# Moving the routing to odd steps, the token sums ahead of their splits, and two stored-square jobs into the next block, in a hand-ordered attention and mixture kernel

## The chip, the cores and the metric

The kernel runs on one core of a Trainium2 chip. The metric is device microseconds for one execution. Three runs of the kernel before gave a median of 723.92 us (723.49 to 724.7).

## The reference

Three layers follow one another on 3072 tokens with 512 features:

```
attention  4 batches, 8 heads, chunks of 32 queries, 8 memory + up to 56 context keys
dense      h = x @ w_in (512 x 2048); g = s * relu(h)^2 + b; y = g @ w_out (2048 x 512)
soft MoE   logits = y @ phi (32 slots); d = softmax over all 3072 tokens; slots = d.T @ y
           8 experts on 4 slots each: relu(slots @ w1[e]) @ w2[e]
           out = softmax over the slots(logits) @ slot_out
```

All data are float32.

## The kernel before

The tokens are cut into six planes of 512 (j = 0 to 5). For the dense layer each float32 operand is split into a high and a low part (ACT writes the high part with a copy, DVE or POOL subtracts it to get the low part), and each product is three matmuls (high x high, high x low, low x high). One matmul has a 128x128 stationary and a 128x512 moving operand.

Planes 0 and 1 run in 32 plain steps (16 tiles of the 2048 middle features for each plane). Step n issues on PE: 12 matmuls of `mm_h(n)` (L326, writes HB[n % 2]), then background work, then 12 matmuls of `mm_y(n-1)` (L345, accumulates in banks 0 to 3). On ACT and DVE `make_g(n)` turns h into the two parts of g, and `split_wi`, `split_wo` make the weights' parts for coming steps (two buffers each, wi0/wi1 and wo0/wo1). The background work is the attention of a later plane and the routing of the plane before, given by the table `bg`. Attention of one head pair is "qk" (32 small matmuls, L192, then exp and norm on DVE and ACT), two steps later "tr" (four transposes L221, `att_place` copies them to pb), one step later "pv" (32 small matmuls L241 and a copy L247). Routing is "log" (logits L371, running maximum, exp), "etr" (two transposes), four "ytr" (four transposes each, L393, and one copy to SBUF), "csoft" (DVE and ACT only) and "slot" (8 matmuls L409). "tr", "qk" and routing alternate over banks 6 and 7 through `mbank()`.

Planes 2 and 3, then 4 and 5, go through `super_block(s)`, s = 0 and 1. There eight pairs of feature tiles, p = 0 to 7, each form h with seven products instead of eight (`prod`, L630, 6 matmuls each, in the order a11, s1, s2, s4, s3, a22, a12 on the four banks A to D). Its operands are the token sums `x_sum` (t1 to t4, built in place from the raw tokens x0h), split by `x_split` into w0 to w13, and the weight sums `w_sums`, split by `w_split`. Two of the four resulting squares are used at once for the first plane's y (two jobs of 12 matmuls L345, run one pair later from the list `pending`), two are stored (x1h, sp0 to sp3). After the pairs come 16 "stored-square jobs" (`t2_job(i)`, L345), 12 matmuls each, for the second plane. `prep(i)` splits the weights and squares for job i: `wo_split` (L635 on ACT, L636 on POOL) and `g_split` (L643 on ACT, L647 on DVE). While the jobs of block 0 run, `tasks` make the sums and splits of block 1. Routing of a finished plane stands at spots (p, k): k = 1 after product s2, k = 2 after product s3; k = 1 uses bank B, k = 2 bank D.

What sets the order: the steps before 28 have PE and SP ordered by hand, with ACT, DVE and POOL placed by a scheduler; from step 28 to the end of both blocks the order of the program is the order on all five queues. Each engine takes its queue strictly in order. The expert layer after the blocks is not touched.

Of the kernel before, what the change touches and what calls it, by code (L numbers as in the profile page):

```python
# [38 lines left out]
def tile_attention_moe_softmoe(  # L39
# [524 lines left out]

    def x_split(op, s, kt):
        j = NPL + 2 * s
        t = hl(fresh(f"w{XO[op] + kt}"))
        src = {"b21": xraw(j, 2 + kt), "b22": xraw(j + 1, 2 + kt), "t3": xraw(j + 1, kt)}.get(op, xraw(j, kt))
        act.activation(out=r32(t[:, 0]), in_=src, func=AF.Copy)
        dve.tensor_tensor(out=r32(t[:, 1]), in0=src, in1=t[:, 0], op=ALU.subtract)  # L570
# [84 lines left out]
    def super_block(s, pending):  # L655
# [106 lines left out]
        if s == 0:  # L762
            for kt in range(2):
                task(1 + kt, x_split, "b11", 1, kt)
                task(1 + kt, x_sum, "t1", 1, kt)
                task(1 + kt, x_split, "t1", 1, kt)
                task(3 + kt, x_sum, "t3", 1, kt)
                task(3 + kt, x_sum, "t2", 1, kt)
                task(4 + kt, x_split, "t2", 1, kt)
                task(6 + kt, x_split, "b22", 1, kt)  # L770
                task(6 + kt, x_sum, "t4", 1, kt)
                task(8 + kt, x_split, "b21", 1, kt)
                task(11 + kt, x_split, "t3", 1, kt)
                task(13 + kt, x_split, "t4", 1, kt)
            task(8, wi_load, 0)
            task(10, w_sums, 0)
# [404 lines left out]
```

## Time and profile before

| | us |
|---|---|
| median of three runs | 723.92 |
| the profiled execution | 728.35 |
| its span on the chip | 726.6 |
| PE busy (modelled) | 673.3 |
| DVE, ACT, POOL busy | 420.5, 380.3, 308.3 |

The stretches of the program in this execution: plain steps 16 to 31 from about 126 to 272 us, pairs of block 0 to 424, its stored-square jobs to 489, pairs of block 1 to 616, its jobs to 670, experts and output to the end. A row of the timeline has start, length, engine, line, operation, output and inputs, and in brackets the idle time of that engine just before with what ended it. PE is the engine to follow: a bracket on a PE row is time lost if nothing later has slack. A matmul row's length includes a latency of the last matmul, so the next row can start a little before the end of the one above.

### The profile page before, as it was taken

The page shows a single profiled execution, that of the slowest core. Times are in us where ns is not written, and L with a number is a line of the kernel's source. Part 1 is how long each engine was busy: PE and PEld are TensorE (multiplying, and loading weights), DVE is VectorE, ACT ScalarE, POOL GpSimd, SP SyncE. Part 2 cuts the span into 40 slices and gives each one's busy share as a digit, 9 for nine tenths or more (in the row PEclk, how much of TensorE's full clock was granted, in tenths as well). Part 3 has the DMA queues.
Part 4 walks back from the last instruction along what each step waited for, and adds up shares of the span by engine and source line. Part 5 has one row for each costly group of instructions (what it writes and reads, how often), then busy time and mean ns, then how long its engine had stood idle before and what let it go on. Part 6 is the DMA issues. An engine that isn't in the chain of part 4 may idle for free.

```text
span 726.6 us, 12554 instructions
## 1 busy us (share of the span) xinstructions
PE 673.3 (93%) x4983; PEld 527.3 (73%) x4983; DVE 420.5 (58%) x692; ACT 380.3 (52%) x688; POOL 308.3 (42%) x261
## 2 busy tenths in 40 slices
PE   6899999988899779999999998888999999999996
PEld 3678887776678666787777886666787887877474
DVE  4799997544454534656655555864354446464423
ACT  3898874544344444554555554536464456353323
POOL 4100001322244475665666436886396674253000
PEclk8999999999899989999999999999999999999998
DMA  8999946641223502433321050003922100999896
GB/s 338 397 373 343 392 146 199 192 152 65 87 88 117 203 29 88 145 132 134 142 88 59 30 203 30 0 30 107 383 71 76 59 30 29 386 353 344 319 361 266
DMA packets 37786, 126.90 MB, mean 175 GB/s; under 512 B 4192, under 2 KB 4192, under 8 KB 37728
## 3 DMA queue, kind: packets, MB, share of 16 engines
q1 hardware_dynamic: 37728, 126.11, 47.1%
q8 instruction: 39, 0.64, 0.4%
q14 instruction: 19, 0.16, 0.1%
HBM read 111.41 MB, written 14.68 MB: 174 GB/s over the span
## 4 chain that ended last, share of the span: by engine, by line
PE 69%; DVE 10%; ACT 6%; POOL 6%; issue 5%; DMA 2%; SPq 0%; DVEq 0%; ACTq 0%; POOLq 0%
PE bank L345 30%; PE bank L630 15%; PE bank L326 9%; PE bank L241 3%; PE bank L192 2%; DVE rt L653 2%; PE bank L1043 2%; PE bank L1002 2%; POOL x00n L576 1%; DMA v<-vd 1%; POOL wo L636 1%; PE bank L393 1%; ACT rt L650 1%; POOL x01n L576 1%; POOL sp6n L603 1%
## 5 line engine op out<-in xcount | busy, mean ns | idle before, releaser
L345 PE MATMUL bank<-g,wo 128*128 128x512 f32 x1008 | 254.4, 403 | 6.1 <-POOL wo L636 4.7
L345 PEld LDWEIGHTS bank<-g,wo 128*128 128x128 f32 x1008 | 188.6, 192 | 52.2 <-POOL wo L636 6.0
L326 PE MATMUL bank<-x,wi 128*128 128x512 f32 x384 | 95.8, 399 | 4.3 <-ACT x03n L247 4.0
L326 PEld LDWEIGHTS bank<-x,wi 128*128 128x128 f32 x384 | 73.5, 193 | 20.7 <-ACT x03n L247 4.5
L636 POOL TENSOR_TENSOR wo<-yt,wo 128x512 fp32r<-128x512 f32 x36 | 49.8, 1387 | 48.5 <-ACT wo L635 48.3
L310 POOL TENSOR_TENSOR wi<-w,wi 128x512 fp32r<-128x512 f32 x16 | 20.5, 1281 | 115.2 <-ACT wi L306 114.0
L333 DVE SCALAR_TENSOR_TENSOR rt<-bank,cons,rt 128x512 f32<-128x512 f32 x32 | 23.9, 747 | 56.2 <-ACT rt L332 56.1
L319 POOL TENSOR_TENSOR wo<-w,wo 128x512 fp32r<-128x512 f32 x16 | 20.8, 1302 | 59.8 <-ACT wo L318 59.8
L623 POOL TENSOR_TENSOR w14n<-sp6n,w14n 128x512 fp32r<-128x512 f32 x16 | 29.6, 1847 | 37.1 <-ACT w14n L622 37.1
L650 ACT ACTIVATE rt1n<-y 128x1024 f32<-128x1024 f32 x16 | 17.0, 1061 | 43.1 <-DVE y L727 43.1
L635 ACT ACTIVATE wo<-yt 128x512 fp32r<-128x512 f32 x36 | 22.7, 631 | 24.8 <-PE bank L345 24.8
L647 DVE SCALAR_TENSOR_TENSOR g<-rt,cons,g 128x512 fp32r<-128x512 f32 x32 | 26.2, 819 | 15.7 <-ACT g L643 15.4
L306 ACT ACTIVATE wi<-w 128x512 fp32r<-128x512 f32 x32 | 20.1, 628 | 27.5 <-PE bank L326 27.5
L318 ACT ACTIVATE wo<-w 128x512 fp32r<-128x512 f32 x32 | 20.2, 632 | 27.2 <-PE bank L345 26.5
L643 ACT ACTIVATE g<-rt,cons 128x512 fp32r<-128x512 f32 x32 | 23.2, 726 | 19.8 <-DVE rt L653 19.8
L192 PEld LDWEIGHTS bank<-k,q 128*64 128x64 f32 x704 | 22.7, 140 | 10.6 <-DVE pb L234 4.1
L241 PEld LDWEIGHTS bank<-pb,v 128*64 128x64 f32 x704 | 23.0, 141 | 10.1 <-issue 4.9
L192 PE MATMUL bank<-k,q 128*64 128x64 f32 x704 | 25.6, 227 | 3.9 <-DVE pb L234 2.2
L725 DVE TENSOR_TENSOR y<-bank,y 128x512 f32<-128x512 f32 x16 | 11.1, 691 | 30.6 <-PE bank L630 30.5
L335 DVE SCALAR_TENSOR_TENSOR g<-rt,cons,g 128x512 fp32r<-128x512 f32 x32 | 25.0, 781 | 6.1 <-ACT g L334 5.5
L653 DVE SCALAR_TENSOR_TENSOR rt<-bank,cons,rt 128x512 f32<-128x512 f32 x16 | 12.0, 750 | 28.2 <-ACT rt L650 28.2
L241 PE MATMUL bank<-pb,v 128*64 128x64 f32 x704 | 26.0, 228 | 1.6 <-DVE x L257 1.4
(487 smaller groups left out, 1541.9 us busy)
## 6 DMA issues: line engine op xcount, KB each, us to landing
sp<-wd SPq DMA_DIRECT2D x24, 512.0 KB, 9.0
k<-kd SPq DMA_DIRECT2D x22, 512.0 KB, 5.7
v<-vd SPq DMA_DIRECT2D x22, 512.0 KB, 4.3
q<-qd SPq DMA_DIRECT2D x20, 512.0 KB, 4.2
yt<-dwo SPq DMA_DIRECT2D x18, 512.0 KB, 3.3
dwi<-w SPq DMA_DIRECT2D x16, 256.0 KB, 7.2
dwo<-w SPq DMA_DIRECT2D x16, 256.0 KB, 6.8
sp4n<-dwi SPq DMA_DIRECT2D x8, 512.0 KB, 3.2
```

What stands on the lines that cost most here:

```text
L192: pe.matmul(S[64 * par:64 * par + 64, 2 * i + z, :], lhsT=qt[:, c].rearrange("p h n -> p (h n)"), rhs=kt[:, c, :], start=True, stop=True)
L241: pe.matmul(b[64 * h:64 * h + 64, 64 * m:64 * m + 64], lhsT=vt[:, m, h, :], rhs=pb[:, m // 2, m % 2, h].rearrange("p z n -> p (z n)"), sta ...
L326: pe.matmul(HB[n % 2], lhsT=r32(w[:, a, kt, :]), rhs=r32(x[:, b]), start=(kt == 0 and i == 0), stop=(kt == 3 and i == 2))
L333: dve.scalar_tensor_tensor(out=t, in0=HB[n % 2], scalar=s_col, in1=r, op0=ALU.mult, op1=ALU.mult)
L335: dve.scalar_tensor_tensor(out=r32(g[:, 1]), in0=t, scalar=b_col, in1=g[:, 0], op0=ALU.add, op1=ALU.subtract)
L345: pe.matmul(yb[dt], lhsT=r32(w[:, a, dt * 128:dt * 128 + 128]), rhs=r32(g[:, b]), start=(first and i == 0), stop=(last and i == 2))
L623: pool.tensor_tensor(out=r32(lo), in0=src, in1=hi, op=ALU.subtract)
L630: pe.matmul(b, lhsT=r32(wv[:, a, kt, :]), rhs=r32(xv[:, c]), start=(first and kt == 0 and i == 0), stop=(kt == 1 and i == 2), skip_group_c ...
L636: pool.tensor_tensor(out=r32(t[:, 1]), in0=src, in1=t[:, 0], op=ALU.subtract)
L647: dve.scalar_tensor_tensor(out=r32(g[:, 1]), in0=t, scalar=b_col, in1=g[:, 0], op0=ALU.add, op1=ALU.subtract)
L650: act.activation(out=r, in_=h, func=AF.Relu, scale=1.0 / WSCALE ** 2)
L653: dve.scalar_tensor_tensor(out=out, in0=h, scalar=s_col, in1=r, op0=ALU.mult, op1=ALU.mult)
```

## The change

1. Routing of plane 0 stands on odd steps (19, 21, 23, 25), beside "pv", instead of even ones (18, 20, 22, 24), beside "tr" and "qk".
2. Steps 28 to 31 have a step of their own, `hand_step`. The split of the weights wi for step n + 2 follows `make_g(n)`; in the old step the split for n + 1 stands at the head of step n. The token sums t2, t3, t4 stand one step ahead of their splits, most of them on DVE instead of POOL; the weight splits of pair 0 are spread over steps 30 and 31. The last "pv" uses bank 7.
3. In a pair, `att_place` stands before `finish`, and the routing spots are one later: (1,1) to (4,1) instead of (0,2) to (3,2).
4. In the stored-square jobs `prep` runs three jobs ahead instead of two, the eight token sums of block 1 move from POOL to DVE one or more jobs before their splits, and the splits are in another order. The raw weights of jobs 10 to 15 swap their tiles.
5. The stored-square jobs 14 and 15 of block 0 run as the two "pending" jobs in pair 0 of block 1, followed by the copy of y to SBUF.

```diff
-    for step, task in ((2, "log"), (2, "ytr0"), (4, "etr"), (4, "ytr1"), (6, "ytr2"), (6, "ytr3"), (6, "csoft"), (8, "slot")):
+    for step, task in ((3, "log"), (3, "ytr0"), (5, "etr"), (5, "ytr1"), (7, "ytr2"), (7, "ytr3"), (7, "csoft"), (9, "slot")):
...
-    WOR = ["yt0", "yt1", "w14", "wi0", "w15", "rt0", "y1", "y0"]
+    WOR = ["yt0", "yt1", "w14", "wi0", "w15", "y0", "y1", "rt0"]
...
-    def x_sum(op, s, kt):
+    def x_sum(op, s, kt, eng=dve):
...
-        pool.tensor_tensor(out=o, in0=a, in1=b, op=ALU.subtract)
+        eng.tensor_tensor(out=o, in0=a, in1=b, op=ALU.subtract)
...
-        routing = {(0, 2): "log", (1, 1): "ytr0", (1, 2): "etr", (2, 1): "ytr1", (2, 2): "ytr2", (3, 1): "ytr3",
-                   (3, 2): "slot"}
+        routing = {(1, 1): "log", (1, 2): "ytr0", (2, 1): "etr", (2, 2): "ytr1", (3, 1): "ytr2", (3, 2): "ytr3",
+                   (4, 1): "slot"}
...
+            if s == 0 and p == 0:
+                x_split("t4", 0, 1)
             if p:
-                finish(p - 1)
                 if s == 0:
                     att_place(4 * NHP + p, D)
+                finish(p - 1)
...
+            for i, op, kt in ((1, "t1", 0), (2, "t1", 1), (4, "t2", 0), (5, "t2", 1), (6, "t3", 0), (7, "t3", 1),
+                              (8, "t4", 0), (9, "t4", 1)):
+                task(i, x_sum, op, 1, kt)
...
+        rest = []
         for i in range(NF):
+            if s == 0 and i >= NF - 2:
+                rest.append(lambda i=i: t2_job(i))
+                continue
             t2_job(i, (3, 2, 0, 1) if i == 0 else (0, 1, 2, 3))
...
+            if i + 3 < NF - 2:
+                prep(i + 3)
+            elif NF - 4 <= i < NF - 2:
+                prep(i + 2)
...
-            if i + 2 < NF:
-                prep(i + 2)
...
+        def hand_step(n):
+            m = n - (NSTEP - 4)
+            if m == 0:
+                split_wi(n + 1)
...
+            split_wo(n)
+            mm_h(n, (0, 1, 2, 3))
+            if m == 3:
+                w_split(1, 0)
+            make_g(n)
+            if n + 2 < NSTEP:
+                split_wi(n + 2)
+            for task, a in bg[n]:
+                run_bg(task, a, bank[7] if n == NSTEP - 1 else HB[(n + 1) % 2] if task == "pv" else mbank())
+            mm_y(n - 1)
+            if m == 0:
+                x_sum("t2", 0, 0, pool)
+                x_sum("t3", 0, 0, pool)
+                x_high("b22", 0, 0)
+            elif m == 1:
+                x_low("b22", 0, 0)
+                x_split("t2", 0, 0)
+                x_split("t3", 0, 0)
+                x_sum("t4", 0, 0)
...
-            super_block(0, [last_plain, lambda: None])
-            super_block(1, [lambda: y_evac(yb=bank[4:8]), lambda: None])
+            rest = super_block(0, [last_plain, lambda: None])
+            super_block(1, [rest[0], lambda: last_jobs(rest[1])])
```

Three places show what this moves. The first is PE in step 18, where the logits (L371) and the first transposes (L393) of the routing stood behind the transposes of the attention (L221, bank 7, `bank_166`) and its "qk" (L192, bank 6, `bank_165`):

```order
 L221 MATMUL bank_166<-cons,ep 128x128 x4
 L192 MATMUL bank_165<-k_102,q_100 64x64 x16
-L371 MATMUL bank_166<-yt_107,cons 32x128 x8
-L371 MATMUL bank_166<-yt_108,cons 32x128 x8
-L393 MATMUL bank_165<-cons,yt_107 128x128 x2
-L393 MATMUL bank_165<-cons,yt_108 128x128 x2
 L345 MATMUL bank_159<-g_96,wo_86 128x512
```

They leave that step, and PE goes from "qk" straight to the job. In step 19 they stand behind "pv" (L241), in the same two banks:

```order
 L326 MATMUL bank_164<-x_94,wi_84 128x512 x3
 L241 MATMUL bank_163<-pb_105,v_103 64x64 x16
+L371 MATMUL bank_166<-yt_107,cons 32x128 x8
+L371 MATMUL bank_166<-yt_108,cons 32x128 x8
+L393 MATMUL bank_165<-cons,yt_107 128x128 x2
+L393 MATMUL bank_165<-cons,yt_108 128x128 x2
 L345 MATMUL bank_159<-g_95,wo_85 128x512
```

One job and one `mm_h` now lie between the users of each bank. The second place is ACT in steps 28 and 29, before. L569 is the high part of an `x_split` (w12 belongs to t4), L306 and L318 are the high parts of the step weights wi and wo, L332 and L334 belong to `make_g`, L247 is the copy of a "pv":

```order
L569 ACTIVATE w8n<-x02n 128x512
L569 ACTIVATE w6n<-x00n 128x512
L569 ACTIVATE w10n<-x00n 128x512
L569 ACTIVATE w12n<-x00n 128x512
L306 ACTIVATE wi_83<-w_81 128x512
L318 ACTIVATE wo_86<-w_80 128x512
L332 ACTIVATE rt_98<-bank_164 128x512
L334 ACTIVATE g_96<-rt_98,cons 128x512
L247 ACTIVATE x03n<-bank_163 128x512
L306 ACTIVATE wi_84<-w_82 128x512
L318 ACTIVATE wo_85<-w_81 128x512
```

The split of t4 stands ahead of the weights of step 30 (`wi_83`) and of the copy x03. Now, from the weights of step 30 on:

```order
L306 ACTIVATE wi_83<-w_81 128x512
L230 ACTIVATE pb_106<-bank_165 64x16x32
L208 ACTIVATE ep<-ep 128x512
L571 ACTIVATE w8n<-x02n 128x512
L318 ACTIVATE wo_86<-w_80 128x512
L332 ACTIVATE rt_98<-bank_164 128x512
L334 ACTIVATE g_96<-rt_98,cons 128x512
L306 ACTIVATE wi_84<-w_82 128x512
L247 ACTIVATE x03n<-bank_163 128x512
L571 ACTIVATE w6n<-x00n 128x512
L571 ACTIVATE w10n<-x00n 128x512
L318 ACTIVATE wo_85<-w_81 128x512
```

The weights and the copy stand ahead of w6 and w10, and w12 is one step later. The third place is DVE in the middle of the stored-square jobs of block 0, before. L647 is the low part of a `g_split`, L570 that of an `x_split`, L397 the copy of a "ytr", L539 belongs to "etr":

```order
L647 SCALAR_TENSOR_TENSOR sp5n<-x12n,cons,sp5n 128x512
L397 COPY w12n<-bank_159 128x512
L647 SCALAR_TENSOR_TENSOR g_96<-x13n,cons,g_96 128x512
L570 TENSOR_TENSOR w6n<-x00n,w6n 128x512
L539 COPY lall<-bank_160 128x128
L647 SCALAR_TENSOR_TENSOR g_95<-x13n,cons,g_95 128x512
L570 TENSOR_TENSOR w7n<-x01n,w7n 128x512
L647 SCALAR_TENSOR_TENSOR sp5n<-sp_112,cons,sp5n 128x512
L570 TENSOR_TENSOR w8n<-x02n,w8n 128x512
L397 COPY w13n<-bank_162 128x512
```

And now, between the same two copies (L575 is the old L570, L656 the old L647, L585 is a token sum):

```order
L397 COPY w12n<-bank_159 128x512
L575 TENSOR_TENSOR w5n<-x01n,w5n 128x512
L585 TENSOR_TENSOR x00n<-x02n,x00n 128x512
L656 SCALAR_TENSOR_TENSOR sp5n<-sp_112,cons,sp5n 128x512
L539 COPY lall<-bank_160 128x128
L575 TENSOR_TENSOR w9n<-x03n,w9n 128x512
L585 TENSOR_TENSOR x01n<-x03n,x01n 128x512
L656 SCALAR_TENSOR_TENSOR g_96<-sp_112,cons,g_96 128x512
L575 TENSOR_TENSOR w6n<-x00n,w6n 128x512
L585 TENSOR_TENSOR x00n<-x02n,x00n 128x512
L656 SCALAR_TENSOR_TENSOR g_95<-sp_113,cons,g_95 128x512
L397 COPY w13n<-bank_162 128x512
```

The sums stand in DVE's own queue, two or more instructions ahead of the split that reads them.

## Rows read from the trace of the kernel before

**Rows 1.** The page: span, and busy time of PE.

```profile
span 726.6 us, 12554 instructions
PE 673.3 (93%) x4983; PEld 527.3 (73%) x4983; DVE 420.5 (58%) x692; ACT 380.3 (52%) x688; POOL 308.3 (42%) x261
```

**Rows 2.** Windows: stretch, length, busy time and instructions of each engine, granted clock.

```profile
core 0: us, PE busy (x) PEld busy (x) DVE busy (x) ACT busy (x) POOL busy (x), PEclk, DMA share, GB/s
143.30:217.33 74.03, 64.61 (x526) 51.40 (x522) 33.37 (x64) 31.02 (x55) 22.00 (x18) 0.93 0.29 101
217.33:238.46 21.13, 21.13 (x181) 17.33 (x177) 10.26 (x16) 9.74 (x16) 10.70 (x9) 1.00 0.30 101
238.46:291.75 53.29, 42.99 (x279) 33.32 (x275) 24.57 (x46) 24.06 (x47) 29.93 (x28) 0.90 0.29 109
291.75:407.31 115.56, 113.20 (x831) 91.30 (x831) 69.33 (x109) 61.23 (x107) 70.91 (x61) 0.99 0.31 110
...
423.71:503.31 79.60, 68.06 (x349) 52.32 (x347) 49.75 (x62) 38.77 (x76) 53.12 (x40) 0.98 0.19 66
503.31:521.11 17.80, 17.62 (x73) 14.04 (x73) 7.80 (x11) 8.62 (x16) 11.79 (x11) 0.90 0.94 363
521.11:616.11 95.00, 94.12 (x417) 75.31 (x417) 48.39 (x58) 52.23 (x88) 63.55 (x55) 1.00 0.20 71
```

**Rows 3.** Timeline of PE, steps 18, 20 and 24.

```profile
151.53 1.08 PE L371 MATMUL bank<-yt,cons 128*32 128x128 f32 x32 [0.97 <-DVE pb L234]
...
171.73 0.66 PE L393 MATMUL bank<-cons,yt 128*128 128x128 f32 x4 [2.00 <-DVE ep L207]
172.14 4.58 PE L345 MATMUL bank<-g,wo 128*128 128x512 f32 x12
...
210.57 3.04 PE L345 MATMUL bank<-g,wo 128*128 128x512 f32 x12
```

**Rows 4.** Timeline of PE, from step 30 to the start of pair 1, block 0.

```profile
252.26 5.49 PE L326 MATMUL bank<-x,wi 128*128 128x512 f32 x12 [4.05 <-ACT x03n L247]
...
271.82 1.39 PE L630 MATMUL bank<-w0n,wi0n 128*128 128x512 f32 x3 [3.72 <-ACT x00n L247]
...
289.95 0.66 PE L221 MATMUL bank<-cons,ep 128*128 128x128 f32 x4 [1.33 <-ACT ets L385]
291.75 0.98 PE L630 MATMUL bank<-w0n,wi0n 128*128 128x512 f32 x3 [1.14 <-DVE rt L653]
```

**Rows 5.** Timeline of ACT in steps 28 and 29.

```profile
248.04 0.63 ACT L569 ACTIVATE w12n<-x00n 128x512 fp32r<-128x512 f32 x1 [3.31 <-POOL x00n L576]
...
251.63 0.58 ACT L247 ACTIVATE x03n<-bank 128x512 f32<-128x512 f32 x1
```

**Rows 6.** Timeline of PE in pair 5 of block 0.

```profile
369.84 0.95 PE L630 MATMUL bank<-w0n,wi0n 128*128 128x512 f32 x3
...
374.79 1.15 PE L192 MATMUL bank<-k,q 128*64 128x64 f32 x32 [0.58 <-DVE pb L234]
...
388.57 0.95 PE L630 MATMUL bank<-w0n,wi0n 128*128 128x512 f32 x3
```

**Rows 7.** Timeline of PE, stored-square jobs of block 0 and pair 1 of block 1.

```profile
447.33 3.02 PE L345 MATMUL bank<-sp5n,wi1n 128*128 128x512 f32 x12 [2.36 <-ACT sp5n L643]
...
471.60 2.88 PE L345 MATMUL bank<-sp5n,rt1n 128*128 128x512 f32 x12
474.32 3.79 PE L345 MATMUL bank<-g,wo 128*128 128x512 f32 x16
...
503.31 0.98 PE L630 MATMUL bank<-w0n,wi0n 128*128 128x512 f32 x3 [2.97 <-DVE rt L653]
```

**Rows 8.** Timelines of DVE and POOL in the same jobs.

```profile
441.53 0.68 DVE L570 TENSOR_TENSOR w1n<-x01n,w1n 128x512 fp32r<-128x512 f32 x1
...
466.50 1.78 DVE L570 TENSOR_TENSOR w9n<-x03n,w9n 128x512 fp32r<-128x512 f32 x1
...
465.99 1.74 POOL L636 TENSOR_TENSOR wo<-rt,wo 128x512 fp32r<-128x512 f32 x1
```

More of the change, by code (lines that the diff above doesn't have):

```diff
@@ L563, in w_store, with x_src, x_high, x_low @@
             sp.dma_start(out=d[p][:, 512 * h:512 * h + 512], in_=W[f][:, 512 * m:512 * m + 512])
-    def x_split(op, s, kt):
[L566 to L570, printed above, removed]
-    def x_sum(op, s, kt):
+    def x_src(op, s, kt):
+        j = NPL + 2 * s
+        return {"b21": xraw(j, 2 + kt), "b22": xraw(j + 1, 2 + kt), "t3": xraw(j + 1, kt)}.get(op, xraw(j, kt))
+    def x_high(op, s, kt):
+        t = hl(fresh(f"w{XO[op] + kt}"))
+        act.activation(out=r32(t[:, 0]), in_=x_src(op, s, kt), func=AF.Copy)
+    def x_low(op, s, kt):
+        t = hl(cur[f"w{XO[op] + kt}"])
+        dve.tensor_tensor(out=r32(t[:, 1]), in0=x_src(op, s, kt), in1=t[:, 0], op=ALU.subtract)
+    def x_split(op, s, kt):
+        x_high(op, s, kt)
+        x_low(op, s, kt)
+    def x_sum(op, s, kt, eng=dve):
         j = NPL + 2 * s
@@ L762, in super_block @@
         if s == 0:
[L763 to L776, printed above, removed]
-            task(10, w_split, 0, 0)
-            task(10, w_split, 1, 0)
-            task(11, w_split, 2, 0)
-            task(11, wi_load, 1)
+            for i, (op, kt) in enumerate((("b11", 0), ("b11", 1), ("b22", 0), ("t1", 0), ("t1", 1), ("b22", 1), ("t2", 0),
+                                          ("t2", 1), ("b21", 0), ("b21", 1), ("t3", 0), ("t3", 1), ("t4", 0), ("t4", 1))):
+                task(i, x_split, op, 1, kt)
+            for i, op, kt in ((1, "t1", 0), (2, "t1", 1), (4, "t2", 0), (5, "t2", 1), (6, "t3", 0), (7, "t3", 1),
+                              (8, "t4", 0), (9, "t4", 1)):
+                task(i, x_sum, op, 1, kt)
+            task(5, wi_load, 0)
+            task(8, w_sums, 0)
+            task(10, w_split, 2, 0)
+            task(11, w_split, 1, 0)
+            task(12, w_split, 0, 0)
+            task(12, wi_load, 1)
         else:
@@ L797, in super_block @@
                 pending.pop(0)()
+                prep(2)
                 ybuf[:] = [fresh(f"w{k}") for k in range(10, 14)]
@@ L806, in super_block @@
                 run_bg("csoft", j1)
-            if i + 2 < NF:
-                prep(i + 2)
             for t in tasks[i]:
                 t()
-        ybuf[:] = SPARE[0:4]
+        return rest
     with tc.manual_schedule(engines={mybir.EngineType.PE, mybir.EngineType.SP}):
@@ L903, in plain_step @@
                 for kt in range(2):
-                    x_sum("t1", 0, kt)
+                    x_sum("t1", 0, kt, pool)
             if n in (NF + 2, NF + 6, NF + 10):
@@ L927, in last_plain, with last_jobs @@
             y_evac()
+        def last_jobs(job):
+            job()
+            ybuf[:] = SPARE[0:4]
+            y_evac(yb=bank[4:8])
         for n in range(NSTEP - 4):
```

28 lines of the change are left out of this document (12 added, 16 removed).

## The prediction

> **What bounds the kernel now.** I read the page first: PE is modelled busy for 673.3 of 726.6 us, DVE, ACT and POOL for 42 to 58% [rows 1]. So PE's order sets the time, and what a change can win is PE's waits, plus matmuls that run slowly behind them. Second, the windows, cut at the stages that the change touches [rows 2]. Two are the reference: 217.33 to 238.46 and 521.11 to 616.11 have PE busy all or 99% of the time at a granted clock of 1.00. The others hold 9.4 us (143 to 217), 10.3 us (238 to 292), 2.4 us (292 to 407) and 11.5 us (424 to 503) without PE work, 33.6 us together, and the clock there is 0.93, 0.90, 0.99 and 0.98. Third, the timeline of PE says what each wait was for [rows 3, 4, 6, 7]. Behind longer waits the clock is at the lower of its two levels (1.2 instead of 2.4 GHz) for a while: 12 matmuls take 4.58 us after a wait of 2.00 us and 5.49 us after one of 4.05 us [rows 3, 4], against 2.72 us from start to start in an undisturbed stretch, from 471.60 to 474.32 [rows 7]. So a wait costs more than its bracket.
>
> The sum therefore doesn't add brackets. For each stretch I take its length before and subtract the length of the same PE work in clean pieces. A job, or an `mm_h`, is J = 2.72 us, one product (6 matmuls) half of that. Two clean steps: 217.33 to 238.46 is even, odd, even, 21.13 us, and the odd step from 210.57 to 217.33 is 6.76 us, so an even and an odd step take (21.13 + 6.76) / 2 = 13.95 us and an even one 7.19 us [rows 2, 3]. A clean pair of block 1: (95.00 - 2.7 for three turns and the slots) / 6 = 15.4 us [rows 2]. A clean pair of block 0: 388.57 - 369.84 = 18.73 us, less its wait of 0.58 us and the latency around it (0.15 us, an estimate), 18.0 us [rows 6]. Routing on PE: the logits 1.1 us [rows 3], a turn of four tiles 0.5 us (between the 0.66 us of its row and the 0.41 us to the next start [rows 3]), the slots like the logits, "etr" 0.3 us (two transposes, half a turn): 1.1 + 4 x 0.5 + 0.3 + 1.1 = 4.5 us, an estimate from these rows.
>
> **Part 1, routing on odd steps.** In an even step the logits wait for the copy to pb (bank 7) and the transposes behind them for the softmax that reads bank 6, both issued in the same step: 0.97 us and 2.00 us are two of seven such waits [rows 3]. On the odd step the last user of each bank was a step ago. What is late next? The following "tr" needs the logits' bank. Between them lie the turn, a job and an `mm_h`, about 6 us; the readers (a copy, a maximum, an exp) stand behind `make_g` and the copy of "pv" on ACT and DVE, which I count as about 4 us. So nothing new waits. The window from 143.30 to 217.33 holds four even and four odd steps with all routing: 4 x 13.95 + 4.5 = 60.3 us against 74.03, a gain of **13.7 us**. Bounds: nothing, if the waits move along, and 13.7.
>
> **Part 2, steps 28 to 31 and pair 0.** PE waits 4.05 us in step 30 for the copy x03 [rows 4]. That copy stood at 251.63 because ACT, in order, had waited 3.31 us for POOL's sum for t4 until 248.04, with the weights of step 30 and `make_g` behind [rows 5]. In the new order these stand ahead, and POOL's two remaining sums come after the weights' low part. Counting ACT forward from 243.1 (w8 starts there as before) at 0.5 to 0.6 us each, x03 is copied at about 247.7 and `mm_h(30)` may start at 248.0, when the job before it ends: 0.2 to 0.3 us of slack. The later steps have more. Clean, the stretch is two odd steps, an even one without "qk" (7.19 - 1.1) and a job: 2 x 6.75 + 6.1 + 2.8 = 22.4 us. Pair 0 is a block 0 pair without "pv" and without one job: 18.0 - 1.1 - 2.8 = 14.1 us. It gets a new wait: the logits no longer lie between s3 and a22, and a22 accumulates on the bank that DVE must first read, about 0.9 us; the square of a22 then frees the bank for the next pair some 0.4 us late. That is 15.4 us, and 37.8 in all against 53.29 [rows 2]: a gain of **15.5 us**. The waits of 3.72, 1.33 and 1.14 us [rows 4] go with it, the last one partly back in that 1.3 us. Bounds: 9 us, if the wait for x03 stays with its slow matmuls (4.05 + 5.49 - 2.88 come back [rows 4, 7]), and 16.8.
>
> **Part 3, pairs 1 to 6 of block 0.** `att_place` now doesn't stand behind the `finish` that waits for DVE, so "qk" loses its 0.58 us [rows 6]; `finish` comes later by two copies, and its job is a stage away. All routing lies here now: 6 x 18.0 + 4.5 = 112.5 us against 115.56, **3.0 us**. Bounds: 0 and 3.0.
>
> **Part 4, stored squares and pair 0 of block 1.** 423.71 to 503.31 is 18 jobs, seven products, routing and a second set of logits: 49.0 + 9.5 + 4.5 + 1.1 = 64.1 us of 79.6 [rows 2]. The waits are for `prep` (2.36 us for a square [rows 7]), held up behind sums on POOL that ACT waits for, and at the end 2.97 us for DVE before pair 1. Three-ahead `prep` has two jobs, 5.4 us, from the release of its buffers; its four instructions need about 2.5 us. Jobs 14 and 15 fill the chains of pair 0, and the logits leave (they are in part 5). I leave 0.5 us for the first product, whose weights' split is now the last one, and 1.5 us for the following cost: 65.0 us, a gain of **14.6 us**.
>
> The eight sums are new work for DVE, in a stage where it shares something with POOL: the low part of a split takes 0.68 us at 441.53, and 1.78 us at 466.50, when POOL's split from 465.99 ran beside it for 1.74 us [rows 8]. DVE has 36 such instructions in these jobs (14 squares, 14 operands, 8 sums). Alone they take 36 x 0.68 = 24 us, all beside POOL 36 x 1.78 = 64 us. POOL has 14 splits left there besides the four weight sums and their splits, so I count 16 at 1.78 and 20 at 0.68, 42 us, and about 6 us of copies and softmax: 48 us, as much as PE's 47.6 (16 jobs and the routing without the products). With three jobs of lead little of that reaches PE, hence 1.5 us. Bounds: 0, and 64 + 6 less the 6 us that can run on into pair 0, less 47.6: 16 us.
>
> The Trainium skill (SBUF — State Buffer, Who interferes with whom) says that a VectorE instruction with two SBUF inputs and a GpSimd instruction that reads SBUF exclude each other, the second to issue waiting for all of the first. By that rule the sums gain a cross-engine wait less and pay with a lock; where every one of them meets a POOL instruction, it gives the 16 us, and where the lock is free the 1.5 us. The row of 1.78 us agrees with it.
>
> **Part 5, the rest of block 1.** Pair 1 was 17.80 us at a clock of 0.90 [rows 2]; clean it is 15.4 with the logits and one turn, 17.0. "etr" moves on to a later pair, 0.3. A gain of **0.5 us**. The jobs of block 1, which have no PE waits to speak of, and the experts shift as a whole; the DMA order there is tied to the same jobs.
>
> **Sum.** 13.7 + 15.5 + 3.0 + 14.6 + 0.5 = 47.3 us. The profiled execution took 728.35 us: 681.0. That is 4.4 us above the median of the runs; the terms are differences of device time, so 723.92 - 47.3 = 676.6, and I forecast **677 us**.
>
> **Rivals.**
> 1. DVE and POOL bound the stored squares. For: the 1.78 us row, and 48 us of DVE work on 47.6 of PE. Against: a lead of three jobs, and POOL with eight instructions less. At the full price part 4 gives nothing back: 677 + 14.5 = 691.5 us.
> 2. The copy x03 is still late in step 30 (slack 0.2 us by my count). Then 6.7 us come back: about 684 us. Against: the copies ahead of it no longer wait for POOL.
> 3. The routing waits move along with it: the next "tr" and "qk" wait for banks 7 and 6. For: the rotation over two banks is unchanged. Against: about 2 us of slack. Part 1 goes: 690.5 us. Two of these rivals together come to about 700.
> 4. Slower. The clock doesn't keep its upper level once PE has no pauses left: between 143 and 521 us PE would work almost without a stop. Its price is 5.49 - 2.88 over 12 matmuls, 0.22 us each [rows 4, 7]; it decides against the change from 47.3 / 0.22 = 215 slow matmuls on, and with 240 of them the time is 729 us. Against: 95 us of unbroken pairs and 21 us of steps ran at 1.00 [rows 2], and every fall seen so far follows a pause.
>
> **How the numbers follow.** Forecast 0.62, rival 1 (at full or half price, 684 to 691) 0.14, rival 2 0.10, rival 3 0.08, two together 0.03, slower 0.02, nothing changed 0.01. No measurement of this kernel tells less than about 0.2%, 1.4 us, from no change; so faster 0.97, same 0.01, slower 0.02. The forecast's own range is 672 to 682. Downwards it ends where the 1.5 us of lock and the 1.3 + 0.5 us of new waits don't appear, 673.3, and the estimated pieces are 2 us too long: 671. Upwards rivals 1 to 3 belong to it, to 691. The range is 671 to 691.
>
> **What would show it.** In the profile after: PE rows of steps 19 to 25 without a bracket, and about 60 us for eight steps; `mm_h(30)` directly behind its job, at a clock of 1.00; a bracket of about 1 us before a22 in pair 0 of block 0; "qk" in pairs 4 to 6 without one; in the stored squares brackets of 2 us together at most, and DVE rows between 0.68 and 1.78 us; jobs inside pair 0 of block 1, and pair 1 of it at 1.00. Wrong would be: brackets that name the copy to pb or a softmax before "tr" or "qk" (rival 3), several on `g_low` or on POOL's split in the squares (rival 1), or a clock under 0.95 in a stretch without waits (rival 4).

## The result and the profile after

The changed kernel took **685.33 us** (median of 4 runs, 684.27 to 687.01) beside 724.06 us for the kernel before: ratio 0.9467, 95% interval 0.9444 to 0.9491. Forecast were 677 us with 671 to 691. The gain is 38.7 us, 8.6 less than the 47.3 of the sum.

The page of the changed kernel, span and PE, beside [rows 1]:

```profile
span 685.2 us, 12578 instructions
...
PE 658.4 (96%) x4983; PEld 518.4 (76%) x4983; DVE 441.3 (64%) x704; ACT 378.8 (55%) x688; POOL 292.1 (43%) x249
```

Its windows, cut at the same instructions as [rows 2]: steps 18 to 25, steps 28 to 31 with pair 0, pairs 1 to 6 of block 0, the 14 jobs that stay in the stored squares, pair 0 of block 1, pair 1, pairs 2 to 7.

```profile
core 0: us, PE busy (x) PEld busy (x) DVE busy (x) ACT busy (x) POOL busy (x), PEclk, DMA share, GB/s
142.94:202.54 59.60, 59.60 (x527) 48.31 (x523) 34.50 (x64) 31.14 (x57) 22.75 (x19) 1.00 0.39 125
...
223.66:265.94 42.28, 37.33 (x246) 29.28 (x243) 34.31 (x45) 22.89 (x43) 27.40 (x23) 1.00 0.27 97
265.94:378.24 112.30, 112.30 (x863) 90.85 (x863) 73.84 (x114) 61.07 (x111) 72.30 (x62) 1.00 0.33 113
...
394.63:443.26 48.63, 48.53 (x251) 38.52 (x250) 41.24 (x53) 29.15 (x55) 25.24 (x19) 1.00 0.27 98
443.26:462.46 19.20, 16.88 (x67) 13.19 (x65) 11.96 (x13) 9.22 (x17) 16.01 (x14) 0.91 0.08 27
462.46:479.63 17.17, 16.99 (x103) 13.44 (x103) 9.71 (x15) 8.99 (x19) 11.35 (x10) 1.00 0.94 368
479.63:575.10 95.47, 94.59 (x419) 75.65 (x420) 49.41 (x60) 52.44 (x89) 63.62 (x55) 1.00 0.21 72
```

| Part | before, us | after, us | gain | forecast |
|---|---|---|---|---|
| 1: steps 18 to 25 | 74.03 | 59.60 | 14.4 | 13.7 |
| 2: steps 28 to 31, pair 0 | 53.29 | 42.28 | 11.0 | 15.5 |
| 3: pairs 1 to 6, block 0 | 115.56 | 112.30 | 3.3 | 3.0 |
| 4: squares, pair 0 of block 1 | 79.60 | 67.83 | 11.8 | 14.6 |
| 5: pair 1; pairs 2 to 7 | 17.80; 95.00 | 17.17; 95.47 | 0.2 | 0.5 |

The rest of the span gave 0.7 us, so the two profiled executions differ by 41.3 us (728.35 to 687.01), the medians by 38.7. Parts 1 and 3 have PE busy from end to end, and the jobs of part 4 as well (48.53 of 48.63 us). The waits that are left lie at four places. The timeline of PE, with the idle time before an instruction and its releaser in brackets:

```profile
233.99 3.04 PE L326 MATMUL bank<-x,wi 128*128 128x512 f32 x12 [0.58 <-ACT x03n L247]
...
251.59 0.96 PE L639 MATMUL bank<-w6n,wi1n 128*128 128x512 f32 x3 [1.88 <-ACT y L711]
...
262.48 0.96 PE L639 MATMUL bank<-w12n,w15n 128*128 128x512 f32 x3 [2.49 <-DVE y L738]
...
446.09 0.79 PE L639 MATMUL bank<-w0n,wi0n 128*128 128x512 f32 x1 [2.21 <-POOL wi0n L632]
```

The first answers the 4.05 us of [rows 4]: 0.58 us are left before `mm_h(30)`, and its 12 matmuls take 3.04 instead of 5.49 us. The other three are the product s2 and the product a22 in pair 0 of block 0, and the first product of pair 0 of block 1.

For s2 the copy of c11 (L711) is late on ACT, which works in order. ACT's timeline there, then DVE's:

```profile
243.60 0.58 ACT L332 ACTIVATE rt<-bank 128x512 f32<-128x512 f32 x1
248.28 0.73 ACT L334 ACTIVATE g<-rt,cons 128x512 fp32r<-128x512 f32 x1 [4.11 <-DVE rt L333]
...
250.95 0.58 ACT L711 ACTIVATE y<-bank 128x512 f32<-128x512 f32 x1
```

```profile
245.09 1.77 DVE L575 TENSOR_TENSOR w12n<-x00n,w12n 128x512 fp32r<-128x512 f32 x1
246.78 0.68 DVE L575 TENSOR_TENSOR w9n<-x03n,w9n 128x512 fp32r<-128x512 f32 x1
247.50 0.75 DVE L333 SCALAR_TENSOR_TENSOR rt<-bank,cons,rt 128x512 f32<-128x512 f32 x1
...
258.57 1.46 DVE L215 TENSOR_TENSOR ep<-ep,ast 128x512 f32<-128x512 f32 x1
259.95 1.27 DVE L364 TENSOR_SCALAR sp<-bank 128x512 f32<-128x512 f32 x2
261.15 0.67 DVE L736 TENSOR_TENSOR y<-bank,y 128x512 f32<-128x512 f32 x1
261.75 0.67 DVE L738 TENSOR_TENSOR y<-bank,y 128x512 f32<-128x512 f32 x1
```

ACT waits 4.11 us for the `rt` of step 31, which stands on DVE behind two low parts; four more instructions stand between that g and the copy of c11. Later, DVE reaches the two adds that a22 needs only behind the attention's row (L215) and two copies of y (L364).

At the end of the stored squares POOL and DVE are both without a pause (POOL, then DVE):

```profile
439.77 1.75 POOL L632 TENSOR_TENSOR w14n<-sp6n,w14n 128x512 fp32r<-128x512 f32 x1
441.48 1.74 POOL L632 TENSOR_TENSOR wi1n<-sp6n,wi1n 128x512 fp32r<-128x512 f32 x1
443.19 1.71 POOL L645 TENSOR_TENSOR wo<-rt,wo 128x512 fp32r<-128x512 f32 x1
444.87 1.17 POOL L632 TENSOR_TENSOR wi0n<-sp4n,wi0n 128x256 fp32r<-128x256 f32 x1
```

```profile
440.29 1.78 DVE L656 SCALAR_TENSOR_TENSOR g<-sp,cons,g 128x512 fp32r<-128x512 f32 x1
442.00 1.78 DVE L575 TENSOR_TENSOR w10n<-x00n,w10n 128x512 fp32r<-128x512 f32 x1
443.70 1.75 DVE L575 TENSOR_TENSOR w11n<-x01n,w11n 128x512 fp32r<-128x512 f32 x1
```

Each engine advances once in 1.70 us. The low part of wi0, which the first product waits for, is the last of POOL's weight splits. Behind that wait the clock falls, 0.91 over the 19.20 us of pair 0.

### The profile page after: what moved, and what is told of

Same layout as the page of the kernel before. It is cut to its first block, busy times and chain, and to the rows that moved or that the text cites. A ratio compares the mean times of both kernels' runs of the same rounds, so it can differ in the third digit from the quotient of the medians.

```text
span 685.2 us, 12578 instructions
## 1 busy us (share of the span) xinstructions
PE 658.4 (96%) x4983; PEld 518.4 (76%) x4983; DVE 441.3 (64%) x704; ACT 378.8 (55%) x688; POOL 292.1 (43%) x249
## 4 chain that ended last, share of the span: by engine, by line
PE 81%; DVE 7%; ACT 4%; POOL 3%; issue 3%; DMA 1%; SPq 0%; DVEq 0%; ACTq 0%; POOLq 0%
PE bank L345 34%; PE bank L639 20%; PE bank L326 10%; PE bank L241 3%; PE bank L192 3%; PE bank L1080 2%; PE bank L1039 2%; PE bank L393 2%; PE bank L221 1%; DMA sp<-wd 1%; DVE rt L662 1%; PE bank L371 1%; PE bank L1109 1%; POOL sp6n L612 1%; PE bank L409 1%
## 5 line engine op out<-in xcount | busy, mean ns | idle before, releaser
L345 PE MATMUL bank<-g,wo 128*128 128x512 f32 x1008 | 248.2, 396 | 0.0
L345 PEld LDWEIGHTS bank<-g,wo 128*128 128x128 f32 x1008 | 184.9, 188 | 42.5 <-issue 2.7
L326 PE MATMUL bank<-x,wi 128*128 128x512 f32 x384 | 93.3, 391 | 0.8 <-ACT x03n L247 0.6
L326 PEld LDWEIGHTS bank<-x,wi 128*128 128x128 f32 x384 | 71.7, 188 | 16.5 <-ACT x03n L247 1.0
L645 POOL TENSOR_TENSOR wo<-yt,wo 128x512 fp32r<-128x512 f32 x36 | 49.4, 1372 | 38.8 <-ACT wo L644 38.7
L656 DVE SCALAR_TENSOR_TENSOR g<-rt,cons,g 128x512 fp32r<-128x512 f32 x32 | 28.0, 873 | 10.2 <-ACT g L652 9.5
L306 ACT ACTIVATE wi<-w 128x512 fp32r<-128x512 f32 x32 | 20.1, 628 | 25.5 <-PE bank L326 25.5
L318 ACT ACTIVATE wo<-w 128x512 fp32r<-128x512 f32 x32 | 20.1, 629 | 24.8 <-PE bank L345 24.1
L652 ACT ACTIVATE g<-rt,cons 128x512 fp32r<-128x512 f32 x32 | 23.2, 725 | 19.2 <-DVE rt L662 19.2
L334 ACT ACTIVATE g<-rt,cons 128x512 fp32r<-128x512 f32 x32 | 23.1, 722 | 13.5 <-DVE rt L333 13.2
L241 PEld LDWEIGHTS bank<-pb,v 128*64 128x64 f32 x704 | 22.9, 141 | 10.1 <-issue 2.8
L192 PEld LDWEIGHTS bank<-k,q 128*64 128x64 f32 x704 | 22.5, 139 | 8.4 <-issue 4.3
L335 DVE SCALAR_TENSOR_TENSOR g<-rt,cons,g 128x512 fp32r<-128x512 f32 x32 | 25.0, 782 | 4.7 <-ACT g L334 4.1
L241 PE MATMUL bank<-pb,v 128*64 128x64 f32 x704 | 25.9, 228 | 1.6 <-DVE x L257 1.4
L192 PE MATMUL bank<-k,q 128*64 128x64 f32 x704 | 25.5, 226 | 1.5 <-DMA k<-kd 1.5
```

The source lines that it names most:

```text
L192: pe.matmul(S[64 * par:64 * par + 64, 2 * i + z, :], lhsT=qt[:, c].rearrange("p h n -> p (h n)"), rhs=kt[:, c, :], start=True, stop=True)
L241: pe.matmul(b[64 * h:64 * h + 64, 64 * m:64 * m + 64], lhsT=vt[:, m, h, :], rhs=pb[:, m // 2, m % 2, h].rearrange("p z n -> p (z n)"), sta ...
L326: pe.matmul(HB[n % 2], lhsT=r32(w[:, a, kt, :]), rhs=r32(x[:, b]), start=(kt == 0 and i == 0), stop=(kt == 3 and i == 2))
L334: act.activation(out=r32(g[:, 0]), in_=t, func=AF.Identity, bias=b_col)
L335: dve.scalar_tensor_tensor(out=r32(g[:, 1]), in0=t, scalar=b_col, in1=g[:, 0], op0=ALU.add, op1=ALU.subtract)
L345: pe.matmul(yb[dt], lhsT=r32(w[:, a, dt * 128:dt * 128 + 128]), rhs=r32(g[:, b]), start=(first and i == 0), stop=(last and i == 2))
```

## The experiments

Times are medians; the intervals are of the ratio to the kernel before in the same set of runs. Besides the medians I compare two stretches of each profile, called A and B (not the banks of that name), since the first 30 us alone differ by up to 1.9 us between runs (last section): **A**, from `mm_h(30)` to the first product of pair 1 of block 0 (31.95 us in the changed kernel, 233.99 to 265.94), and **B**, from a22 of pair 7 of block 0 to the first product of pair 1 of block 1 (70.55 us, 391.91 to 462.46).

**The changed kernel again** (e12_after_again).

> The changed kernel itself, beside the three runs of this call, so that steps of about 1 us can be read on one chip: 685 to 686 us by either theory; its stretches from step 17 on within 0.3 us of the first profile (42.3 us for steps 28 to 31 with pair 0, 67.8 us for the squares with block 1's pair 0), any difference from the first 30 us.

686.44 us (0.9486, 0.9463 to 0.9510). A is 31.92 us. B is 69.09 us, 1.5 less than in the first profile, which I had not expected: the wait is the same, but the matmuls behind it are not slow this time.

```profile
445.11 0.50 PE L639 MATMUL bank<-w0n,wi0n 128*128 128x512 f32 x1 [2.19 <-POOL wi0n L632]
```

So B is good to 1.5 us where this wait stands in it, and A to 0.1 in these two profiles (one later run has slow matmuls in A too).

**Part 1 alone** (e1_odd_only), in the kernel before:

```diff
-((2, "log"), (2, "ytr0"), (4, "etr"), (4, "ytr1"), ..., (8, "slot"))
+((3, "log"), (3, "ytr0"), (5, "etr"), (5, "ytr1"), ..., (9, "slot"))
```

> The kernel before with the one line on routing in the steps (odd instead of even), nothing else of the change. If the waits of steps 18 to 25 come only from where the routing stands, this alone gives what the trace of the changed kernel showed for that stretch, 14.4 us: about 709.6 us (708 to 711), eight steps in about 60 us and no bracket in them. If the gain there needs the other edits too (fewer instructions of POOL, other order), or the waits pass to the next transposes, 715 to 724 us. The stretch from 238 us on stays as it was either way (about 53 us to the end of pair 0).

711.58 us (0.9836, 0.9807 to 0.9866). From step 17's job at 142.93 to step 25's at 202.53 there is no bracket: 59.60 us, the same as in the changed kernel to 0.01. The rest stayed, as the wait for x03 of [rows 4] shows:

```profile
237.45 5.49 PE L326 MATMUL bank<-x,wi 128*128 128x512 f32 x12 [4.04 <-ACT x03n L247]
```

Part 1 is independent of the other edits. The median gains 12.5 us, a little less than the 13 to 16 us expected, the stretch in the profile 14.4 (the baseline, below, may explain the difference). Parts 2 and 3 were not run alone.

**Squares two ahead** (e2_two_ahead), as before:

```diff
-                prep(2)
...
-            if i + 3 < NF - 2:
-                prep(i + 3)
-            elif NF - 4 <= i < NF - 2:
+            if i + 2 < NF:
                 prep(i + 2)
```

> The changed kernel, but the stored squares are split two jobs ahead as before, behind the operands' sums and routing, not three. Theory: the lead is what keeps PE from waiting; one job's square with a lock takes up to 1.75 us on POOL and 1.75 on DVE behind ACT, so brackets on the low parts come back in the 14 jobs: 4 to 10 us slower, 689 to 695 us. Rival: it was the sums that left POOL; then the lead is spare and the time stays within 1 us of the changed kernel (685).

686.31 us (0.9489, 0.9457 to 0.9522), B 70.47 us. The expected loss did not come. Two waits move into the jobs (1.66 and 0.37 us), and the one in the first product shrinks to 0.63 us:

```profile
436.01 2.14 PE L345 MATMUL bank<-sp5n,rt1n 128*128 128x512 f32 x8 [1.66 <-POOL rt1n L645]
...
445.66 0.50 PE L639 MATMUL bank<-w0n,wi0n 128*128 128x512 f32 x1 [0.63 <-POOL wi0n L632]
```

A lead of three only shifts the place where PE meets POOL's queue; my theory that it is what keeps PE from waiting falls.

**Block 1's sums on POOL** (e3_sums_pool), everything else as changed:

```diff
-                task(i, x_sum, op, 1, kt)
+                task(i, x_sum, op, 1, kt, pool)
```

> The changed kernel, but the eight sums of block 1's operands are on POOL again; their places, a step ahead of their splits, and the squares three ahead stay. If place and lead matter and not the engine, 684 to 687 us: POOL gets 8 instructions of 1.3 to 1.75 us, 10 to 14 us, in a stage where it has 24 us of squares in 48. If the lock on DVE is what costs at the end of the squares, 1 to 3 us faster (682 to 684). If the sums must be off POOL, as the change has it, brackets on POOL in the jobs or a longer one in the first product: 688 to 693 us.

691.30 us (0.9555, 0.9523 to 0.9586), B 73.84 us, 3.3 or 4.8 more than in the two profiles of the changed kernel. Eight rows of 1.3 to 1.8 us more keep POOL busy from 418 us on but for one pause of 1.7 us, and the wait for the same low part grows:

```profile
441.66 5.06 PE L345 MATMUL bank<-g,wo 128*128 128x512 f32 x20 [1.11 <-POOL wo L645]
...
450.36 0.50 PE L639 MATMUL bank<-w0n,wi0n 128*128 128x512 f32 x1 [3.16 <-POOL wi0n L632]
```

Here the engine of the sums counts, though they stand a step ahead: POOL's queue is the bound of this stretch, not DVE's.

**Jobs 14 and 15 in the squares again** (e4_no_defer):

```diff
-            if s == 0 and i >= NF - 2:
-                rest.append(lambda i=i: t2_job(i))
-                continue
...
-            super_block(1, [rest[0], lambda: last_jobs(rest[1])])
+            super_block(1, [lambda: last_jobs(lambda: None), lambda: None])
```

> The changed kernel, but jobs 14 and 15 run in the stored squares again and none stands inside pair 0 of block 1. Theory: two opposite things. POOL gets 5.4 us more before the first product, so that bracket of 2.2 us with its slow matmuls goes (minus 3 us); pair 0 gets waits before a22 and before pair 1's first product, 3 to 4 us with the clock. Sum within 1.5 us of the changed kernel: 684 to 687 us, with pair 0 longer and the jobs without a bracket at their end. Rival: the first product's bracket comes from the order of the splits and stays; then 688 to 690 us.

687.24 us (0.9494, 0.9468 to 0.9521), B 71.11 us. The first product's bracket is gone, and others stand in the last jobs and before a22:

```profile
448.37 2.56 PE L345 MATMUL bank<-g,wo 128*128 128x512 f32 x10 [1.16 <-DVE g L656]
...
458.51 0.96 PE L639 MATMUL bank<-w12n,w15n 128*128 128x512 f32 x3 [0.79 <-DVE y L738]
```

As the theory had it, two things nearly cancel, but not where it had them: three of the new waits (0.64, 0.48 and 1.16 us) stand in the last jobs, where it expected none. The deferral is worth 0.6 to 2.0 us in B, no more. Lead, sums and deferral, taken back one at a time, make up 4 to 8 of the 11.8 us of part 4 if they add (an estimate from the stretches B); what the rest comes from, perhaps that the sums stand ahead of their splits, was not run alone.

**wi0's split first** (e5_wi0_first):

```diff
-            task(10, w_split, 2, 0)
+            task(10, w_split, 0, 0)
             task(11, w_split, 1, 0)
-            task(12, w_split, 0, 0)
+            task(12, w_split, 2, 0)
```

> The changed kernel, but the splits of the first pair's stored weights are issued in the order in which PE needs them: the a11 half (wi0) behind square 13 instead of last, the sums' second set (w14, for s4 and s3) last. Theory: the bracket of 2.21 us in a11 is only that wi0's low part stands last in POOL's full queue; ahead of two others of 1.7 us it lands at about 442, before a11 at 443. Gain 2.2 us and the slow matmuls behind it, 3.0 to 3.5 us: about 682 us, no bracket in a11, s1 or s4. Rival: POOL and DVE hold each other up from 430 to 448 and the same lateness comes out in another place (s1 or the jobs): within 1 us of the changed kernel.

682.57 us (0.9419, 0.9393 to 0.9445), B **66.58 us**: 4.0 less than the changed kernel's profile with slow matmuls behind the wait, 2.5 less than the one without. POOL is as full as before, only its order differs; no bracket is left in the stretch.

```profile
437.95 1.18 POOL L632 TENSOR_TENSOR wi0n<-sp4n,wi0n 128x256 fp32r<-128x256 f32 x1
```

```profile
441.43 0.84 PE L639 MATMUL bank<-w0n,wi0n 128*128 128x512 f32 x3
```

It does not come out elsewhere: PE needs the two splits behind it 1.4 and 7 us later than this one. Part 4 is with this 63.9 us (67.83 - 3.97).

**The job of step 31 in halves** (e6_half_jobs); the split of wo that rewrites its weights moves behind the second half:

```diff
-        def last_plain():
-            mm_y(NSTEP - 1)
-            ybuf[:] = SPARE[0:4]
-            y_evac()
+        def last_half(h):
+            n = NSTEP - 1
+            mm_job(YB, WO[n % 2], G[n % 2], False, True, (2 * h, 2 * h + 1))
+            if h:
+                ybuf[:] = SPARE[0:4]
+                y_evac()
...
-            rest = super_block(0, [last_plain, lambda: None])
+            rest = super_block(0, [lambda: last_half(0), lambda: last_half(1)])
```

> The changed kernel, but the job of step 31 is cut in two inside pair 0 of block 0: half of its banks before s4, half between s3 and a22, with the copies of y behind the second half (and one split of wo moved behind it). Theory: a22's bracket of 2.49 us has two parts, PE having nothing between s3 and a22, and DVE making y's copies (1.27 us) before the two adds; both go, and half a job (1.36 us) covers what is left: 2.2 to 2.5 us off, about 683 us, a22 with a bracket under 0.3 us. Rival: DVE is late by the attention's row (1.46 us) and not by the order: then a bracket of 1 us or more stays, 0.5 to 1.3 us off.

686.45 us (0.9471, 0.9443 to 0.9500), A 32.24 us: nothing gained, less than either expectation. a22's bracket halves, and pair 1 gets a new one, since DVE now makes the copies of y ahead of the square that frees the bank.

```profile
259.62 0.96 PE L639 MATMUL bank<-w12n,w15n 128*128 128x512 f32 x3 [1.27 <-DVE y L739]
...
264.58 0.96 PE L639 MATMUL bank<-w0n,wi0n 128*128 128x512 f32 x3 [1.49 <-DVE rt L662]
```

**The two low parts behind g** (e7_lows_later):

```diff
-                x_split("t4", 0, 0)
-                x_split("b22", 0, 1)
+                x_high("t4", 0, 0)
+                x_high("b22", 0, 1)
...
             make_g(n)
+            if m == 3:
+                x_low("t4", 0, 0)
+                x_low("b22", 0, 1)
```

> The changed kernel, but the two low parts on DVE (t4 and b22, 1.77 and 0.68 us at 245.09 and 246.78) are issued behind the g of step 31 instead of ahead of it. Theory: ACT waited 4.11 us until 248.28 for that g, and with it the copy of c11 that s2 waits 1.88 us for; the g comes 2.4 us earlier and s2's bracket goes: 1.9 us off, about 683.4 us. Rival: ACT is then held by POOL or DVE at the next row (the sum for t4, the weights' low part); the bracket shrinks by under 1 us or comes back in s4 or a22: within 0.7 us of the changed kernel.

686.38 us (0.9466, 0.9437 to 0.9496), so no gain in the median. s2's bracket falls from 1.88 to 1.21 us, not to zero, because ACT's next row, a copy to x00, now waits 1.50 us for the low part that still reads x00. a22's is as it was, but in this profile the matmuls behind it are slow (clock 0.64 from 260.10 to 264.90), so A is 32.60 us; without those 1.3 us it would be about 31.3, 0.7 under the changed kernel:

```profile
260.10 1.16 PE L639 MATMUL bank<-w12n,w15n 128*128 128x512 f32 x3 [2.50 <-DVE y L738]
261.05 1.48 PE L639 MATMUL bank<-w13n,w15n 128*128 128x512 f32 x3
```

**All three** (e8_all_three):

> The three edits of the runs beside this one together (wi0's split first, the job of step 31 in halves, the two low parts behind g). If the three places are independent the gains add: 3 + 2.3 + 1.9 = 7.2 us, about 678 us, the value that was forecast for the changed kernel within 1 us. If two of them are one cause (DVE late in pair 0 of block 0 through one chain) the sum falls short by 1.5 to 2.5 us: 680 us.

681.79 us (0.9409, 0.9383 to 0.9435): A 31.56, B 66.59 us, so 0.4 and 2.5 to 4.0 us under the changed kernel. Neither of the two expected values came (678 and 680): the two edits in A bring only these 0.4 us, and brackets of 1.20, 1.26 and 1.50 us stay there. That fits DVE being late as the one cause of s2's and a22's waits, but does not show it.

**y on ACT** (e9_y_on_act), with wi0's split first:

```diff
-            if dt % 2 and not (halve and dt == 3):
+            if not alone and dt % 2 and not (halve and dt == 3):
...
-            y_evac()
+            y_evac(alone=True)
```

> The kernel of e5_wi0_first, and the two copies of y that DVE makes in pair 0 of block 0 (1.27 us, ahead of the adds that a22 waits for) go to ACT, which waits 3.65 us there. Theory now, after the halves of the job only passed the wait on (a22's bracket 2.49 to 1.27 us, and 1.49 us new before pair 1's first product): DVE's queue in this pair holds as much work as PE, so only work taken off DVE counts. Then a22's bracket falls by 1.2 us with none new before pair 1, and the time by as much: 681.4 us against 682.6. Rival: the order of the adds is what counts and ACT's copies are late for pair 1's square instead: bracket moved, same time as e5_wi0_first within 0.4 us.

**681.64 us** (0.9426, 0.9404 to 0.9448; the changed kernel in the same set 0.9486), A 30.74 us. Two copies off DVE take 1.2 us off A (31.95 us in the run of wi0's split first), by the size forecast, and nothing new stands before pair 1. The ratios of the two runs, 0.9426 and 0.9419, are too coarse to show it:

```profile
260.61 0.98 PE L639 MATMUL bank<-w12n,w15n 128*128 128x512 f32 x3 [1.28 <-DVE y L738]
```

Against the halves of the job, which changed the order and left DVE its work, this says that DVE's work in pair 0 is the cost of about half of a22's wait (2.46 to 1.28 us).

**Everything together** (e10_pair0): all edits from wi0's split on, the split of w14 behind the copy of c11, and pair 0's two splits of wo behind its squares.

> All that pointed to a gain together: wi0's split first, the low parts behind g, the job of step 31 in halves, all four copies of y on ACT, the split of the sums' second set (w14) issued behind the copy of c11, and pair 0's two splits of wo behind its squares. Theory (DVE's queue, and c11's copy late on ACT): s2 waits 0.7 us or less (1.20 in e8), a22 0.3 to 0.8 (1.26), pair 1's first product 0.3 or less (1.50): 2 to 3 us under e8_all_three (681.8): 679 to 680 us. Rival: ACT, now with the copies, is the next bound: brackets on ACT before pair 1's products of 1 us or more, 681 to 682 us.

683.80 us (0.9447, 0.9423 to 0.9470). The interval overlaps with that of y on ACT alone, but the profile shows where it is worse: A is 30.50 us, B 66.61, and between the two (from pair 1's first product to pair 7's a22) lie 128.08 us against 125.85. ACT's queue now makes pair 0's square late, so that pair 1 starts late, and pair 1 itself waits:

```profile
249.82 0.97 PE L639 MATMUL bank<-w6n,wi1n 128*128 128x512 f32 x3 [0.68 <-ACT y L711]
...
263.93 0.96 PE L639 MATMUL bank<-w0n,wi0n 128*128 128x512 f32 x3 [1.43 <-DVE rt L662]
...
281.68 0.96 PE L639 MATMUL bank<-w12n,w15n 128*128 128x512 f32 x3 [1.13 <-DVE y L740]
```

The rival was right here (`rt` in the second row waits for ACT's relu for 1.66 us).

**The sums of steps 29 to 31 on POOL** (e11_hand_pool), with wi0's split first:

```diff
-                x_sum("t2", 0, 1)
-                x_sum("t3", 0, 1)
+                x_sum("t2", 0, 1, pool)
+                x_sum("t3", 0, 1, pool)
...
-                x_sum("t4", 0, 1)
+                x_sum("t4", 0, 1, pool)
```

(the sum for t4 of step 29 likewise)

> The kernel of e5_wi0_first, but the five sums that DVE makes in steps 29 to 31 (1.22 to 1.77 us each beside POOL's splits) are on POOL again, at the same places in the order. If DVE's load is the cost in these steps, it loses about 8 us of rows, the g of step 31 is early and the brackets before s2 and a22 (1.88 and 2.46) go, 2 to 4 us off: 679 to 681 us. If a sum on POOL makes ACT wait (as in the kernel before, 3.31 us for the sum of t4), a bracket of 2 to 5 us comes back in step 30, 31 or the first products and takes the gain or more: 683 to 688 us.

682.67 us (0.9430, 0.9405 to 0.9454), A 30.70 us, 1.2 less than with DVE. s2 has no bracket, s1 one of 1.11 us for POOL, a22 still 2.02:

```profile
232.76 3.04 PE L326 MATMUL bank<-x,wi 128*128 128x512 f32 x12 [0.58 <-ACT x03n L247]
...
248.68 0.50 PE L639 MATMUL bank<-w4n,wi1n 128*128 128x512 f32 x1 [1.11 <-POOL wi1n L632]
...
260.00 0.97 PE L639 MATMUL bank<-w12n,w15n 128*128 128x512 f32 x3 [2.02 <-DVE y L738]
```

No wait came back in step 30, its bracket is the same 0.58 us: it was not the engine of the sums that cured x03. That leaves their place behind the weights, which was not run alone. DVE's load is part of A's loss, but a22's wait does not go with it, so neither number of my expectation fits alone.

**y on ACT** has the lowest median measured, 4.8 us under the changed kernel in the same set; its interval overlaps with those of wi0's split first, of all three edits and of the sums on POOL, so the medians do not tell these four apart. y on ACT and the sums on POOL together were not tried.

## Where the prediction was right, and where its sum was wrong

**Direction and mechanism were right.** The measured time lies in the stated range of 671 to 691 us, but that is partly luck: it is outside the forecast's own 672 to 682, in the part that was added for rivals 1 to 3, and none of these came at its price. PE's waits at the named places went, and the clock is 1.00 wherever no wait is left. Steps 19 to 25 show no bracket; "qk" shows none; pair 1 of block 1 runs at 1.00. Rival 3 did not come (part 1 alone gives the whole 14.4 us), rival 4 neither: from 263 to 443 us PE works without a bracket at 1.00. Rival 2 came in small: 0.58 us instead of the slack of 0.2 to 0.3 us. ACT waited 2.12 us for the `rt` of step 29, which stands on DVE behind the attention's row, and the copy of x03 stands behind that g; I had not put this wait into the count forward of ACT. The row took 1.75 us with POOL's split from 229.69 beside it, 0.69 us in a run where it stood alone (279.74 in e10_pair0). So DVE's rows are stretched beside POOL in steps 28 to 31 too, where the prediction had no term for it. ACT's row, then DVE's:

```profile
232.22 0.73 ACT L334 ACTIVATE g<-rt,cons 128x512 fp32r<-128x512 f32 x1 [2.12 <-DVE rt L333]
```

```profile
229.77 1.75 DVE L215 TENSOR_TENSOR ep<-ep,ast 128x512 f32<-128x512 f32 x1
```

**Part 2, short by 4.5 us**, is the larger miss. The step that failed is "it gets a new wait ... about 0.9 us" with 0.4 us for the square: I followed PE's own chain through pair 0 and took DVE and ACT to be free when it called. They were not. The steps took 23.2 us instead of 22.4, and the pair 19.1 us (246.83 to 265.94) against 14.1 clean and 1.3 of waits; s2's 1.88 us had no term at all, and a22's was 2.49. The experiments tell the share of order from that of load: a third of s2's wait is the place of two low parts (1.88 to 1.21), 1.2 us of a22's are two copies that ACT can make; changing only the order of PE gives nothing. With the sums on POOL s2's bracket is gone, but 1.11 us stand before s1 and 2.02 before a22. With the sums on DVE 0.7 us or more are left at s2 and 0.8 at a22 in every run, and the cause of this rest stays open.

**Part 4, short by 2.8 us.** The term "0.5 us for the first product" was the one mis-sized: 2.21 us and, in the profiled execution, 1.5 us of slow matmuls. That the split was "now the last one" I had read from the order; I did not add up what stood ahead of it on POOL. With that one split moved the stretch is 63.9 us. The forecast's 65.0 are 63.0 of clean work (64.1 without the 1.1 us of logits that leave) and 2.0 of waits, so the waits are then nearly gone and the clean pieces were about 0.9 us too short. The 1.5 us for the lock in the jobs did not appear there at all (48.53 of 48.63 us busy). DVE's load was well counted: 48 us forecast, 48.5 busy from 394.63 to 450.60, where its unbroken work ends. But the lock's cost is not spread evenly: two windows of the changed kernel, with the columns as above, have POOL busy for a third of the first and both engines for nearly all of the second, and the last split in there pays:

```profile
394.63:430.00 35.37, 35.27 (x190) 28.49 (x189) 27.98 (x43) 20.41 (x40) 12.27 (x9) 1.00 0.32 120
430.00:448.00 18.00, 15.79 (x69) 11.74 (x68) 18.00 (x15) 10.50 (x20) 17.71 (x13) 0.94 0.09 30
```

Rival 1 named the right pair of engines; its price was worked out as a mean over the stage and is paid in its last third.

The Trainium skill (SBUF — State Buffer, Who interferes with whom) has a VectorE instruction with two SBUF inputs and a GpSimd one that reads SBUF shut each other out. The traces agree in direction: beside POOL's splits DVE's rows take 1.78 instead of 0.68 us. For the size the rows decide: a pair of instructions advances in 1.70 us here, less than the 0.68 of [rows 8] and POOL's 1.28 (278.16, last section) added up. By these rows the two overlap in part; POOL's times in the profile are rough.

**The baseline, 2.6 us.** I subtracted differences read from an execution of 728.35 us from a median of 723.92. The runs of the kernel before, listed with their clocks, span 720.36 us (0.985) over 724.18 (0.976) to 727.79 (0.969); the profiled one has 0.971. So its stretches probably held more slow matmuls behind waits than the median's, and the change can't give back at the median what only that execution had paid. That the clock makes up the whole 2.6 us is inferred, not shown: there is one profile of the kernel before.

The account: 47.3 - 4.5 - 2.8 + 0.7 (part 1) + 0.3 (part 3) - 0.3 (part 5) + 0.7 (the rest) = 41.4, within rounding the 41.3 us of the profiles; less 2.6 is 38.7.

## What to carry to other kernels

When a wait of the bounding engine is removed, count the queues of the engines that feed it through the same stretch, instruction by instruction: a place where they hold as much work as it does gets the next wait, and there a change of order pays only for the instruction that the bounding engine needs first. Issue splits in the order of their use; one such exchange gave 2.5 to 4.0 us here, more than the lead or the deferral. Moving work to an engine that is already full costs as much (3.3 to 4.8 us for the sums on POOL). Subtract differences from the execution they were read in, and ask how its clock stands to the median's before carrying them over.
